# First chunk transposed as fp32 and split into halves on the way out of PSUM, weight slabs in one piece each in DRAM, opening reordered

## The chip, the cores and the metric

The kernel runs on one core of a Trainium2 chip. A core has five engines with instruction queues of their own: TensorE (PE) for matmuls, VectorE (DVE), ScalarE (ACT), GpSimd (POOL) and SyncE (SP), which here issues nearly all DMA transfers. [...] SBUF is the on-chip memory; PSUM holds what TensorE writes, in banks of 128 x 512 fp32.

The metric is the time of one execution in microseconds. Before the change three runs gave 449.02, 449.00 and 449.44 us, median 449.02.

## The reference

Two branches work on the same layer-normalised input and their results are added to it.

```python
xn = (x - mean(x)) / sqrt(var(x) + 1e-5)          # x: 2048 x 448, over the last axis
a  = irfft2(rfft2(xn) * (w_r + 1j * w_i))         # a filter in the frequency domain
b  = (relu(xn @ W_gate) * (xn @ W_up)) @ W_down   # 448 -> 1792 -> 448
out = x + a + b
```

All of it is fp32. The kernel keeps that accuracy with fp16 matmuls: every operand is split into a high half `hi` and a low half `lo`, and a product is hi·hi + lo·hi + hi·lo.

## The kernel before

**Tiling.** The 2048 rows are 16 tiles of 128; tile `n2 = q + 4j` belongs to chunk `q`, so a chunk is four tiles, 512 rows. The chunks are worked on in the order `CHUNKS = [0, 2, 1, 3]`. For each chunk there is a transposed operand `T[q]` (in the records `T_62` for chunk 0) with eight contraction tiles of 128: 0 to 2 hold the high half of the first 384 features, 4 to 6 the low half, and 3 and 7 share the last 64 features, high and low. A ninth tile `Tl` is gathered by small SBUF-to-SBUF transfers (`t_ninth`); the forward transform needs it.

**The gated part.** The 1792 hidden features are 14 slabs `f` of 128, in three groups of 5, 5 and 4. A unit (f, q) of `gu` is two banks, gate (g = 0) and up (g = 1), with ten 128x512 matmuls each (L731), and a pair of units shares four matmuls on half the array (L738, the "halves"). When it is done, ScalarE takes the relu of the gate (L768), VectorE multiplies it by the up bank (L772), ScalarE makes the high half (L776), VectorE the low half (L780). The weights of a slab come as two transfers `wst` (L226) of 256 KB; ScalarE sums their squares (L186), GpSimd reduces over partitions (L189), VectorE makes a scale from it in two steps (L192, L196), ScalarE writes the high half (L681), VectorE the low half (L685). The down projection (`dn`, L799) follows per group and row tile, and VectorE adds its PSUM to the output (L805), which frees the bank. There are two banks each for `gu`, `dn` and `fx` (transforms and transposes).

**The first chunk.** Its rows are loaded (`lx`, L220), VectorE takes the statistics (`st`), ScalarE a square root (`sq`), VectorE makes the reciprocal in five small steps (`rs`), and normalises (`xn`, L293). ScalarE writes the f16 high half from the raw rows (`hi`, L300), GpSimd copies the last 64 columns about (`cp`, L306 and L307), VectorE makes the f16 low half (`lo`, L317 and L318). TensorE transposes eight f16 tiles per row tile against an f16 identity `id_t` (`tpA`, `tpB`, L332), and VectorE or ScalarE copies them out of PSUM into `T` (`vev`, `aev`, L340 and L338). Meanwhile TensorE runs matmuls on a cleared tile (`warm`, 19 of them, and `kw` 1, 6, 3; L1049), whose result is not used. Unit 0 is done in parts of 256 columns (`hh`, `lh`, `hl`, then the gate's or up's number and the half of the chunk), so that it can begin when half of the chunk is there. Chunk 2 goes the old way in both kernels: f16 halves and a transposing DMA (`dm`).

**What sets the order.** The first part is written out by hand: the string `OPENING` names pieces, and each engine's queue gets its share of them in that order (`wsq`, `par`, `wsc`, `whi`, `wlo` for a slab's weight steps, `wdq` for the square sums of the down projection's weights, `re`, `tm`, `gh`, `gl` for the four steps after a unit, `hp` for the halves). Everything behind it is issued unit by unit. A list `bg` holds the transforms, each item with a cost in us on VectorE, and between units as many items are issued as a credit worked out from these costs allows; a scheduler then orders each engine's queue by priorities. Its order also follows what stands in the opening. In the inverse transform a butterfly (L404, L405, L427, L428) feeds a `swap`, two transfers that reverse partitions (L529, L530), and a `pair` (L535, L536) takes the swapped data; in between, rows that need no swap come by small transfers (`y<-row`, L592).

Of the kernel before, what the change touches and what calls it, by code (L numbers as in the profile page):

```python
# [9 lines left out]
F16 = mybir.dt.float16  # L10
F32 = mybir.dt.float32
# [19 lines left out]
lx0 lx4 lw lid lw lx8 lx12 lw lw lw lw lx2 lx10 lx6 lx14 lwd0 lwd1 lwd2 lwd3 lwd4 warm st0 st4 sqA rsA hi4  # L31
xn4 xn0 wsqW0g0 cp4 st8 hi0 parW0g0 st12 wsqW0g1 cp0 tpA0 lo0 tpA4 kw1 wscW0g0 sqB tpB0 kw6 parW0g1 wsqW1g0
rsB whiW0g0 vevB0 lo4 wsqW1g1 xn12 tpB4 kw3 hi8 parW1 wscW0g1 xn8 whiW0g1 cp8 vevA0 vevA4 hi12 tpA8 vevB4
hh10 hh00 lo8 wsqW2g1 cp12 tpA12 hl00 lo12 aevA12 tpB8 aevA8 hl10 wloW0g0 lw aevB8 tpB12 wscW1 lh00 aevB12
wloW0g1 lw lfd hh01 hh11 whiW1g0 st2 lh01 lh10 whiW1g1 hl01 wloW1g0 lw hl11 wsqW2g0 wloW1g1 lw ly0 ly4 ly8
ly12 lh11 wsqW3g0 st10 parW2 hp0 st14 wsqW3g1 gu1g0 st6 wdq0 parW3 wscW2 sqC wscW3 whiW2g0 rsC gu1g1 re0
wloW2g0 whiW3g1 tm0 whiW2g1 xn6 wsqW4g0 xn2 gu2g0 wloW2g1 hi2 re1 xn10 gh0 wloW3g1 whiW3g0 tm1 gu2g1 wdq1
wloW3g0 hi10 xn14 lo2 hi14 hi6 cp14 hp2 wsqW4g1 cp2 lo6 gu3g0 cp10 dm2 lo14 re2 parW4 wdq2 cp6 wscW4 tm2
whiW4g0 dm14 lo10 wdq4 gu3g1 wloW4g0 gh1 dm10 gl0 whiW4g1 gl1 dm6 gu4g0 re3 wloW4g1 wdq3 tm3 wdp gh3
wdsc gh2 gu4g1 gl2 wdh1 wdh2 wdl1 wdh0 wdl2 hp4 gl3 re4 wdh3 tm4 wdl0 gh4 wdh4 gl4 wdl3 wdl4  # L40
# [42 lines left out]
def _constants():  # L83
# [55 lines left out]
    ident = np.eye(128, dtype=np.float16)  # L139
# [5 lines left out]
def tile_gfnet_reglu(ctx: ExitStack, tc: tile.TileContext, x, xr, wgu, wd, wf, ident, c_fd, c_fm, c_im, c_row, c_id,  # L145
# [59 lines left out]
    id_t = ft([128, 128], F16, "id_t")  # L205
# [10 lines left out]
    def load_xr(n2):  # L216

        xr_b[n2] = free.pop(0)
        xr_t[n2] = xr_b[n2].rearrange("p g c k -> p (g c k)")[:, 0:D]
        nc.sync.dma_start(xr_t[n2], xrv[:, n2, :])  # L220
# [34 lines left out]
    rst = {}  # L255
# [21 lines left out]
    for t in tts:  # L277
        G.memset(t[:, 7, 48:64], 0.0)
    for q in CHUNKS:
        G.memset(Tl[q][32:64], 0.0)  # L280

# [4 lines left out]
    def ln_xn(n2, act=False):  # L286
        xn_b[n2] = free.pop(0)
        xn[n2] = xn_b[n2].rearrange("p g c k -> p (g c k)")[:, 0:D]
        r, nm, mean = rst[n2 % 4, n2 // 4]
        if act:  # L290
            A.activation(xn[n2], xr_t[n2], AF.Identity, scale=r, bias=nm)
        else:
            V.tensor_scalar(xn[n2], xr_t[n2], mean, r, op0=OP.subtract, op1=OP.mult)  # L293

    def ln_hi(n2, fused=False):
        new_tt(n2)
        o = tt[n2].rearrange("p a b -> p (a b)")[:, 0:D]
        r, nm, _ = rst[n2 % 4, n2 // 4]
# [29 lines left out]
    def ln_tp(n2, tiles):  # L328
        if n2 not in tp:
            tp[n2] = fx().bitcast(F16).rearrange("p (a b) -> p a b", b=128)  # L330
        for a in tiles:
            P.transpose(tp[n2][:, a, :], tt[n2][:, a, :], id_t)  # L332

    def ln_ev(n2, a0, a1, act):
        q, j = n2 % 4, n2 // 4
        o = Tq[q][:, a0:a1, 128 * j:128 * (j + 1)]
        if act:
            last["A"] = A.activation(o, tp[n2][:, a0:a1], AF.Copy).ins  # L338
        else:
            last["V"] = V.tensor_copy(o, tp[n2][:, a0:a1]).ins  # L340


    def t_ninth(q):

        T = Tq[q]
        with tc.issue_after(last.get("R", last["S"])):
            for r in range(3):
                nc.sync.dma_start(Tl[q][16 * r:16 * (r + 1)], T[112:128, 4 + r])
            nc.sync.dma_start(Tl[q][64:128], T[64:128, 3])
# [701 lines left out]
    pieces = {"lid": lambda: nc.sync.dma_start(id_t, ident), "lfd": lambda: nc.sync.dma_start(fd_t, c_fd),  # L1051
# [8 lines left out]
    for c, q in enumerate(CHUNKS[:2]):  # L1060
        for js, tag in (((0, 1), "A"), ((2, 3), "B")) if c == 0 else (((0, 1, 2, 3), "C"),):
            piece("sq" + tag, ln_sd, q, js)
            piece("rs" + tag, ln_rstd, q, js, c == 0)
        for j in range(4):
            n2 = q + 4 * j
            for tag, fn, *a in (("lx", load_xr), ("ly", load_x), ("st", ln_stats, j), ("xn", ln_xn),
                                ("hi", ln_hi, c == 0), ("cp", ln_copy), ("lo", ln_lo), ("dm", ln_dma),
                                ("tpA", ln_tp, (0, 1, 2)), ("tpB", ln_tp, (4, 5, 6, 3, 7))):
                piece(f"{tag}{n2}", fn, *((q,) if tag == "st" else (n2,)), *a)
            for act in range(2):  # L1070
                piece(f"{'va'[act]}evA{n2}", ln_ev, n2, 0, 3, bool(act))
                piece(f"{'va'[act]}evB{n2}", ln_ev, n2, 3, 8, bool(act))
# [7 lines left out]
    for f in groups[0]:  # L1080
# [5 lines left out]
        piece(f"wscW{f}", w_scale, f)  # L1086
# [4 lines left out]
        for g in range(2):  # L1091
# [4 lines left out]
            if f == 0:  # L1096
                piece(f"parW{f}g{g}", w_sum, f, (g,))
                piece(f"wscW{f}g{g}", w_scale, f, (g,))
# [77 lines left out]
def _arrays(A_x, A_w_r, A_w_i, B_W_gate, B_W_up, B_W_down):  # L1176
# [9 lines left out]
    wgu = np.ascontiguousarray(np.stack([wtiles(B_W_gate), wtiles(B_W_up)], axis=2))  # L1186
# [30 lines left out]
```

## Time and profile before

| | |
|---|---|
| runs | 449.02, 449.00, 449.44 us (median 449.02) |
| profiled execution | 449.44 us, its span 447.6 us |
| TensorE busy | 437.9 us (98%), granted clock 0.998 |
| VectorE busy | 387.2 us (87%) |
| ScalarE busy | 186.7 us (42%) |
| GpSimd busy | 28.8 us (6%) |
| DMA | 39.54 MB, mean 88 GB/s |

The span is the time from the first to the last instruction in the trace; the execution has 1.84 us around it. A row of a timeline has the start in us, the duration, the engine, the line, the operation with its tiles, and in brackets how long the engine had been idle and what released it; `x6` is a run of six such instructions with their common duration. Busy shares are averages over stages with different limits, so the rows of a stage count, not the page's total.

### The profile page before, as it was taken

How to read it: one execution, taken by the hardware profiler on the slowest of the kernel's cores; microseconds unless marked ns; L12 is line 12 of the kernel's file. 1: busy time of each engine (PE TensorE's matmuls, PEld its weight loads, DVE VectorE, ACT ScalarE, POOL GpSimd, SP SyncE). 2: the span in 40 equal slices, each digit the busy share in tenths (PEclk: the TensorE clock that was granted, in tenths of full speed). 3: DMA queues.
4: the chain of work that ended last, by engine and by line, in shares of the span. 5: the costliest groups of instructions: out<-in, count | busy, mean ns of one | idle time of the engine just before them, and what ended most of it. 6: DMA issues, size and time to landing. Idle time of an engine off the chain costs nothing.

```text
span 447.6 us, 7353 instructions
## 1 busy us (share of the span) xinstructions
PE 437.9 (98%) x2616; PEld 218.8 (49%) x2616; DVE 387.2 (87%) x958; ACT 186.7 (42%) x398; POOL 28.8 (6%) x77
## 2 busy tenths in 40 slices
PE   6999999999999999999999999999999999999996
PEld 2644645545445444444444444444445555555653
DVE  5999779777969998999999999999789799699753
ACT  5896263742553955133124255344214134134230
POOL 4220020200100140000000000000000000000000
PEclk9999999999999999999999999999999999999999
DMA  7828985400001272412220210001011211211212
GB/s 259 313 68 246 320 334 105 96 0 22 2 1 48 95 243 74 132 54 72 84 84 2 83 41 1 1 1 61 23 41 55 68 34 56 89 34 48 94 63 82
DMA packets 37756, 39.54 MB, mean 88 GB/s; under 512 B 16550, under 2 KB 33624, under 8 KB 37720
## 3 DMA queue, kind: packets, MB, share of 16 engines
q1 hardware_dynamic: 37720, 39.09, 28.0%
q8 instruction: 20, 0.33, 0.3%
q14 instruction: 16, 0.13, 0.1%
HBM read 24.38 MB, written 3.67 MB: 63 GB/s over the span
## 4 chain that ended last, share of the span: by engine, by line
PE 52%; DVE 38%; DMA 3%; issue 3%; ACT 2%; POOL 1%; SPq 1%; DVEq 0%; ACTq 0%; POOLq 0%
PE gu L731 26%; PE dn L799 12%; DVE g L772 3%; DVE h L780 3%; DVE wt L685 3%; DVE xy L805 2%; PE fx L630 2%; PE fx L649 2%; DVE y L502 2%; DVE y L503 2%; DVE y L405 2%; DVE y L404 2%; DMA sw<-y 2%; DVE y L427 2%; PE gu L738 2%
## 5 line engine op out<-in xcount | busy, mean ns | idle before, releaser
L731 PE MATMUL gu<-T,wt 128*128 128x512 f16 (+1 forms) x1140 | 255.0, 375 | 0.0
L731 PEld LDWEIGHTS <-wt 128*128 128x128 f16 x1140 | 108.8, 98 | 128.3 <-issue 8.5
L799 PE MATMUL dn<-wdt,h 128*128 128x448 f16 x624 | 127.1, 352 | 0.3 <-DVE xy L805 0.3
L799 PEld LDWEIGHTS <-h 128*128 128x128 f16 x624 | 60.3, 98 | 57.7 <-issue 1.1
L776 ACT ACTIVATE h<-g 128x512 f16<-128x512 f32 x56 | 35.0, 627 | 78.8 <-DVE g L772 78.6
L768 ACT ACTIVATE g<-gu 128x512 f32<-128x512 f32 x56 | 33.0, 589 | 73.7 <-PE gu L738 52.1
L772 DVE SCALAR_TENSOR_TENSOR g<-gu,g 128x512 f32<-128x512 f32 x56 | 38.2, 682 | 4.2 <-ACT g L768 4.2
L780 DVE TENSOR_TENSOR h<-g,h 128x512 f16<-128x512 f32 x56 | 38.2, 683 | 3.1 <-ACT h L776 2.6
L805 DVE SCALAR_TENSOR_TENSOR xy<-dn,dsc,xy 128x448 f32<-128x448 f32 x44 | 29.8, 678 | 6.2 <-PE dn L799 6.2
L614 ACT ACTIVATE vt<-y,fsc 128x456 f16<-128x456 f32 x16 | 10.8, 672 | 29.9 <-PE fx L630 17.4
L681 ACT ACTIVATE wt<-wst,wsc 128x512 f16<-128x512 f32 x28 | 19.0, 714 | 6.2 <-DVE wsc L196 6.2
L189 POOL PARTITION_ALL_REDUCE wm<-wm x15 | 9.3, 617 | 181.9 <-ACT junk L186 161.8
L654 DVE SCALAR_TENSOR_TENSOR xy<-fx,fsc,xy 128x448 f32<-128x448 f32 x16 | 10.9, 679 | 11.0 <-PE fx L649 10.9
L685 DVE SCALAR_TENSOR_TENSOR wt<-wst,wsc,wt 128x512 f16<-128x512 f32 x28 | 20.2, 744 | 0.1
L738 PE MATMUL gu<-T,wt 64*128 64x512 f16 x112 | 17.0, 381 | 1.6 <-DVE g L772 1.4
L535 DVE TENSOR_TENSOR y<-y,sw 128x228 f32<-128x228 f32 x32 | 12.4, 388 | 6.8 <-DMA sw<-y 4.1
L186 ACT ACTIVATE junk<-wst 128x512 bf16<-128x512 f32 x28 | 17.4, 622 | 1.3 <-DMA wst<-in_wgu 1.0
L405 DVE TENSOR_TENSOR y<-y,y 128x456 f32<-128x456 f32 x22 | 13.8, 628 | 1.7 <-DMA row<-y 1.4
L392 DVE TENSOR_TENSOR Xh<-X,Xh 128x456 f16<-128x456 f32 x16 | 9.9, 626 | 5.8 <-ACT Xh L389 5.7
L404 DVE TENSOR_TENSOR y<-y,y 128x456 f32<-128x456 f32 x22 | 13.8, 628 | 0.4
L630 PE MATMUL fx<-im,vt 128*128 128x128 f16 x192 | 13.5, 219 | 0.0
L389 ACT ACTIVATE Xh<-X 128x456 f16<-128x456 f32 x16 | 9.2, 577 | 10.1 <-DVE X L387 8.9
(128 smaller groups left out, 476.2 us busy)
## 6 DMA issues: line engine op xcount, KB each, us to landing
sw<-y SPq DMA_DIRECT2D x64, 112.2 KB
wst<-in_wgu SPq DMA_DIRECT2D x28, 256.0 KB
wf<-in_wf SPq DMA_DIRECT2D x16, 228.0 KB
y<-in_xr SPq DMA_DIRECT2D x16, 224.0 KB
xy<-in_x SPq DMA_DIRECT2D x16, 224.0 KB
out<-xy SPq DMA_DIRECT2D x15, 224.0 KB
wdst<-in_wd SPq DMA_DIRECT2D x14, 224.0 KB
fm<-in_c_fm SPq DMA_DIRECT2D x4, 256.0 KB
```

The lines of the kernel that those rows point to most:

```text
L404: V.tensor_tensor(t, a, b, op=OP.add)
L405: V.tensor_tensor(b, a, b, op=OP.subtract)
L630: P.matmul(o, v[:, h, w], m[:, c, :], start=(i == 0), stop=(i == 2), skip_group_check=True)
L685: V.scalar_tensor_tensor(w[:, 4:8, :], st, sc, w[:, 0:4, :], op0=OP.mult, op1=OP.subtract)
L731: last["P"] = P.matmul(hps[f, q][:, g, cs], wt[f, g][:, a, :], Tq[q][:, b, cs], start=(start and i == 0), stop=(stop and i == len(seq) - 1 ...
L738: m = P.matmul(hps[f, q][:, g, 0:512], wt[f, g][rows, 7, :], Tq[q][rows, b, :], start=start, stop=not start).ins
L768: last["A"] = A.activation(g1s[f, q], hps[f, q][:, 0, :], AF.Relu, scale=2.0 ** -22).ins
L772: last["V"] = V.scalar_tensor_tensor(g1, hps[f, q][:, 1, :], 2.0 ** -22, g1, op0=OP.mult, op1=OP.mult).ins
L776: A.activation(ht[f, q][:, 0, :], g1s[f, q], AF.Copy)
L780: V.tensor_tensor(h[:, 1, :], g1s.pop((f, q)), h[:, 0, :], op=OP.subtract)
L799: last["P"] = P.matmul(ps[:, 0:D], ht[f, q][:, a, js], wdt[f][:, b, :], start=(i == 0), stop=(i == n - 1)).ins
L805: last["V"] = V.scalar_tensor_tensor(xy[:, n2, :], dps[n2][:, 0:D], dsc[:, g:g + 1], xy[:, n2, :], op0=OP.mult, op1=OP.add).ins
```

## The change

**First chunk.** The normalised rows are written as fp32 into the memory of the f16 tiles (`xw`), VectorE as before; ScalarE copies the last 64 columns a second time behind them (`xd`). TensorE transposes four fp32 tiles per row tile (16 instead of 32 in all) against an fp32 identity (64 KB instead of 32). ScalarE writes the high half out of PSUM (`th`, 128x4x128, and `tu`, 64x128), and VectorE the low half as PSUM minus high half (`tl`, 128x3x128, and `tv`, 64x128). The f16 halves, the GpSimd copies and the f16 evacuations of this chunk are gone. Tile 7 of `T` now gets its missing rows by three more small transfers in `t_ninth`, and is cleared ahead by one more memset of 32x512; the four memsets of the f16 tiles move behind the transposes.

**Weights.** `wgu` is laid out slab by slab and half by half, so that a transfer of 256 KB reads one piece of DRAM.

**Order.** The identity is loaded from ScalarE's queue. The five steps of the reciprocal and the two of the scale are pieces of their own, and `OPENING` is another string. On TensorE it gives: 20 warm-ups, 8 transposes, 9 warm-ups, 3 matmuls of 128x256, 8 transposes, 37 matmuls of 128x256, where it was 19 warm-ups, then transposes in groups of 3 to 6 with warm-ups or matmuls of 128x256 between them.

Three places, in each engine's queue. First ScalarE in the opening, from unit 0's first high half on; `wt` is a weight's high half, `junk,wm` a square sum, `T_62` the transposed chunk. Before:

```order
L681 ACTIVATE wt<-wst,wsc 128x512
L186 ACTIVATE junk,wm<-wst 128x512
L300 ACTIVATE tt_105<-y_72,rs 128x448
L681 ACTIVATE wt<-wst,wsc 128x512
L300 ACTIVATE tt_106<-y_73,rs 128x448
L186 ACTIVATE junk,wm<-wst 128x512
L338 ACTIVATE T_62<-fx 128x3x128 x2
L338 ACTIVATE T_62<-fx 128x5x128 x2
L681 ACTIVATE wt<-wst,wsc 128x512 x2
```

After, same place:

```order
L356 ACTIVATE T_62<-fx 64x128
L354 ACTIVATE T_62<-fx 128x4x128
L342 ACTIVATE tt_106<-tt_106 128x64
L342 ACTIVATE tt_105<-tt_105 128x64
L190 ACTIVATE junk,wm<-wst 128x512
L708 ACTIVATE wt<-wst,wsc 128x512
L190 ACTIVATE junk,wm<-wst 128x512
L356 ACTIVATE T_62<-fx 64x128
L354 ACTIVATE T_62<-fx 128x4x128
```

All four tiles now leave PSUM through ScalarE, in pairs of a small and a large piece, where it took two of the four before.

Second, ScalarE around 30 us, ahead of slab 4's high half, the last `wt` in each list (`wdm` is a square sum of the down projection's weights, `g` the relu of a unit). Before:

```order
L681 ACTIVATE wt<-wst,wsc 128x512
L186 ACTIVATE junk,wdm<-wdst 128x448
L302 ACTIVATE tt_104<-y_84 128x448
L302 ACTIVATE tt_105<-y_85 128x448
L302 ACTIVATE tt_106<-y_82 128x448
L186 ACTIVATE junk,wm<-wst 128x512
L768 ACTIVATE g_513<-gu 128x512
L186 ACTIVATE junk,wdm<-wdst 128x448
L681 ACTIVATE wt<-wst,wsc 128x512
```

After:

```order
L190 ACTIVATE junk,wdm<-wdst 128x448
L708 ACTIVATE wt<-wst,wsc 128x512
L306 ACTIVATE tt_104<-y_79 128x448
L803 ACTIVATE h<-g_394 128x512
L306 ACTIVATE tt_105<-y_81 128x448
L190 ACTIVATE junk,wm<-wst 128x512
L190 ACTIVATE junk,wdm<-wdst 128x448
L306 ACTIVATE tt_106<-y_80 128x448
L190 ACTIVATE junk,wdm<-wdst 128x448
L795 ACTIVATE g_489<-gu 128x512
L708 ACTIVATE wt<-wst,wsc 128x512 x2
```

The high half now stands behind three square sums of the down projection in this stretch, where it stood behind two, and directly behind the relu.

Third, VectorE where the inverse transform first needs swapped data, near 316 us (`y<-y,sw` are the pairs, `g` a gate product, `xy<-dn` the evacuation of the down projection). Before:

```order
L588 TENSOR_SCALAR row<-fx,small 16x4x57 x2
L780 TENSOR_TENSOR h<-g_3465,h 128x512
L535 TENSOR_TENSOR y_77<-y_77,sw_1904 128x4x57
L536 TENSOR_TENSOR y_77<-y_77,sw_1904 128x4x57
L602 TENSOR_TENSOR y_70<-y_77 128x228
L603 TENSOR_TENSOR y_77<-y_77 128x228
L604 TENSOR_TENSOR y_77<-y_77 128x114
L772 SCALAR_TENSOR_TENSOR g_3506<-gu,g_3506 128x512
L605 TENSOR_TENSOR y_77<-y_77 128x114
L535 TENSOR_TENSOR y_79<-y_79,sw_1905 128x4x57
L536 TENSOR_TENSOR y_79<-y_79,sw_1905 128x4x57
L805 SCALAR_TENSOR_TENSOR xy<-dn,dsc,xy 128x448
```

After:

```order
L613 TENSOR_SCALAR row<-fx,small 16x4x57 x2
L453 SCALAR_TENSOR_TENSOR y_81<-y_70,y_81 128x456
L807 TENSOR_TENSOR h<-g_3446,h 128x512
L560 TENSOR_TENSOR y_77<-y_77,sw_1885 128x4x57
L561 TENSOR_TENSOR y_77<-y_77,sw_1885 128x4x57
L832 SCALAR_TENSOR_TENSOR xy<-dn,dsc,xy 128x448
L799 SCALAR_TENSOR_TENSOR g_3487<-gu,g_3487 128x512
L560 TENSOR_TENSOR y_83<-y_83,sw_1886 128x4x57
L561 TENSOR_TENSOR y_83<-y_83,sw_1886 128x4x57
```

The evacuation moved up, to directly behind the first pair. Some 30 instructions later in the same queue the gate product of the next unit stood like this before, the pair with `sw_1904` being the one that waited 18 instructions ahead of it:

```order
L535 TENSOR_TENSOR y_74<-y_74,sw_1904 128x4x57
L536 TENSOR_TENSOR y_74<-y_74,sw_1904 128x4x57
L780 TENSOR_TENSOR h<-g_3649,h 128x512
L602 TENSOR_TENSOR y_77<-y_75 128x228
L805 SCALAR_TENSOR_TENSOR xy<-dn,dsc,xy 128x448
```

and stands like this after, one row ahead of the pair with the same swap (`sw_1885`):

```order
L645 SCALAR_TENSOR_TENSOR vt_1882<-y_83,fsc,vt_1882 128x456
L628 TENSOR_TENSOR y_75<-y_75 128x228
L560 TENSOR_TENSOR y_81<-y_81,sw_1888 128x4x57
L561 TENSOR_TENSOR y_81<-y_81,sw_1888 128x4x57
L799 SCALAR_TENSOR_TENSOR g_3630<-gu,g_3630 128x512
L560 TENSOR_TENSOR y_74<-y_74,sw_1885 128x4x57
```

The product moved from behind that pair to ahead of it.

The diff, cut to its core (of `OPENING` the first line of each):

```diff
 OPENING = """
-lx0 lx4 lw lid lw lx8 lx12 lw lw lw lw lx2 lx10 lx6 lx14 lwd0 lwd1 lwd2 lwd3 lwd4 warm st0 st4 sqA rsA hi4
...
+lx0 lx4 lw st0 lx8 lx12 lw lw lw lwd2 lid lw lw lwd0 st4 lwd1
...
-    ident = np.eye(128, dtype=np.float16)
+    ident = np.eye(128, dtype=np.float32)
...
-    id_t = ft([128, 128], F16, "id_t")
+    id_t = ft([128, 128], F32, "id_t")
...
-        eng.dma_start(wst[f, g], wgu[f, :, g])
+        eng.dma_start(wst[f, g], wgu[f, g])
...
-    for t in tts:
-        G.memset(t[:, 7, 48:64], 0.0)
     for q in CHUNKS:
         G.memset(Tl[q][32:64], 0.0)
+    G.memset(Tq[CHUNKS[0]][32:64, 7], 0.0)
...
-    def ln_tp(n2, tiles):
-        if n2 not in tp:
-            tp[n2] = fx().bitcast(F16).rearrange("p (a b) -> p a b", b=128)
-        for a in tiles:
-            P.transpose(tp[n2][:, a, :], tt[n2][:, a, :], id_t)
-
-    def ln_ev(n2, a0, a1, act):
+    xw = {CHUNKS[0] + 4 * j: t.rearrange("p a b -> p (a b)").bitcast(F32) for j, t in enumerate(tts)}
+
+    def ln_xw(n2, act=False):
+        r, nm, mean = rn[n2 % 4, n2 // 4]
+        if act:
+            A.activation(xw[n2][:, 0:D], xr_t[n2], AF.Identity, scale=r, bias=nm)
+        else:
+            V.tensor_scalar(xw[n2][:, 0:D], xr_t[n2], mean, r, op0=OP.subtract, op1=OP.mult)
+
+    def ln_xd(n2):
+        A.activation(xw[n2][:, 448:512], xw[n2][:, 384:448], AF.Copy)
+
+    def ln_tp(n2):
+        tp[n2] = fx().rearrange("p (a b) -> p a b", b=128)
+        for a in range(4):
+            P.transpose(tp[n2][:, a, :], xw[n2][:, 128 * a:128 * (a + 1)], id_t)
+        G.memset(tts[n2 // 4][:, 7, 48:64], 0.0)
+
+    def ln_thi(n2, part):
         q, j = n2 % 4, n2 // 4
-        o = Tq[q][:, a0:a1, 128 * j:128 * (j + 1)]
-        if act:
-            last["A"] = A.activation(o, tp[n2][:, a0:a1], AF.Copy).ins
+        T, js = Tq[q], slice(128 * j, 128 * (j + 1))
+        if part == 0:
+            A.activation(T[:, 0:4, js], tp[n2], AF.Copy)
         else:
-            last["V"] = V.tensor_copy(o, tp[n2][:, a0:a1]).ins
-
+            last["A"] = A.activation(T[64:128, 7, js], tp[n2][64:128, 3], AF.Copy).ins
+
+    def ln_tlo(n2, part):
+        q, j = n2 % 4, n2 // 4
+        T, js = Tq[q], slice(128 * j, 128 * (j + 1))
+        if part == 0:
+            V.tensor_tensor(T[:, 4:7, js], tp[n2][:, 0:3], T[:, 0:3, js], op=OP.subtract)
+        else:
+            last["V"] = V.tensor_tensor(T[64:128, 3, js], tp[n2][64:128, 3], T[64:128, 7, js], op=OP.subtract).ins
...
                 nc.sync.dma_start(Tl[q][16 * r:16 * (r + 1)], T[112:128, 4 + r])
+                if q == CHUNKS[0]:
+                    nc.sync.dma_start(T[16 * r:16 * (r + 1), 7], T[112:128, r])
...
-    pieces = {"lid": lambda: nc.sync.dma_start(id_t, ident), "lfd": lambda: nc.sync.dma_start(fd_t, c_fd),
+    pieces = {"root": lambda: A.activation(mt([128, 1], F32, "root"), eps, AF.Sqrt),
+              "lid": lambda: nc.scalar.dma_start(id_t, ident), "lfd": lambda: nc.sync.dma_start(fd_t, c_fd),
...
-    wgu = np.ascontiguousarray(np.stack([wtiles(B_W_gate), wtiles(B_W_up)], axis=2))
+    wgu = np.ascontiguousarray(np.stack([wtiles(B_W_gate), wtiles(B_W_up)], axis=1))
```

More of the change, by code (lines that the diff above doesn't have):

```diff
@@ L253, in ln_stats @@
         V.bn_aggr(mv[q][:, j, :], st)
-    rst = {}
+    rst, rn = {}, {}
     def ln_sd(q, js=(0, 1, 2, 3)):
@@ L297, in ln_hi @@
         o = tt[n2].rearrange("p a b -> p (a b)")[:, 0:D]
[L298 removed]
+        r, nm, _ = rn[n2 % 4, n2 // 4]
         if fused:
@@ L1085, in tile_gfnet_reglu @@
         piece(f"parW{f}", w_sum, f)
-        piece(f"wscW{f}", w_scale, f)
+        for k in range(2):
+            piece(f"wscW{f}.{k}", w_scale, f, (0, 1), k)
         for tag, fn in (("re", gu_relu), ("tm", gu_times), ("gh", gu_hi), ("gl", gu_lo)):
@@ L1097, in tile_gfnet_reglu @@
                 piece(f"parW{f}g{g}", w_sum, f, (g,))
-                piece(f"wscW{f}g{g}", w_scale, f, (g,))
+                for k in range(2):
+                    piece(f"wscW{f}g{g}.{k}", w_scale, f, (g,), k)
                 for h in range(2):
```

75 lines of the change are left out of this document (40 added, 35 removed).

## Prediction

> **What bounds the kernel now.** I read the page first: the busy line, the granted clock, the shares of the chain that ended last, and the two matmul groups that show any idle time.
>
> ```profile
> span 447.6 us, 7353 instructions
> ...
> PE 437.9 (98%) x2616; PEld 218.8 (49%) x2616; DVE 387.2 (87%) x958; ACT 186.7 (42%) x398; POOL 28.8 (6%) x77
> ...
> PEclk9999999999999999999999999999999999999999
> ...
> PE 52%; DVE 38%; DMA 3%; issue 3%; ACT 2%; POOL 1%; SPq 1%; DVEq 0%; ACTq 0%; POOLq 0%
> ...
> L799 PE MATMUL dn<-wdt,h 128*128 128x448 f16 x624 | 127.1, 352 | 0.3 <-DVE xy L805 0.3
> ...
> L738 PE MATMUL gu<-T,wt 64*128 64x512 f16 x112 | 17.0, 381 | 1.6 <-DVE g L772 1.4
> ```
>
> TensorE is busy for 98% of the span at a full granted clock, so the time is TensorE's work plus the few places where TensorE has nothing to do. Idle time in the middle is 0.3 and 1.6 us. Then I cut the span into stretches, with each engine's busy time in each.
>
> ```profile
> 0.00:20.00 20.00, 15.80 (x105) 9.14 (x105) 14.63 (x48) 13.73 (x29) 6.86 (x25) 1.00 0.86 293
> ...
> 40.00:160.00 120.00, 120.00 (x740) 60.67 (x739) 99.37 (x276) 60.21 (x130) 12.70 (x29) 1.00 0.38 113
> 160.00:310.00 150.00, 150.00 (x742) 68.21 (x740) 145.66 (x326) 57.48 (x136) 5.95 (x12) 1.00 0.20 61
> 310.00:340.00 30.00, 28.32 (x148) 13.36 (x147) 25.52 (x65) 8.31 (x14) 0.00 (x0) 1.00 0.12 39
> ```
>
> The columns after the length are busy time on TensorE, its weight loads, VectorE, ScalarE and GpSimd. From 40 to 310 us TensorE never stops; from 160 to 310 VectorE is full too (145.66 of 150). So the change can act in two places: in the first 20 us, where TensorE still runs warm-up matmuls and waits for the first chunk, and around 310 to 340 us, where 30 − 28.32 = 1.7 us are lost. The matmuls of the two projections and the transforms stay as they are in number and shape.
>
> **The opening, term by term.** The rows are the timeline's: start, busy time, engine, line.
>
> ```profile
> 0.74 0.24 POOL L278 MEMSET tt<- 128x16 f16 x4 [0.29 <-POOLq L1205]
> ...
> 1.03 1.90 POOL L280 MEMSET Tl<- 32x512 f16 x4
> ...
> 3.58 6.97 PE L1049 MATMUL dn<-warm 128*128 128x512 f16 x19 [3.58 <-POOL warm L1106]
> ...
> 10.93 0.44 PE L332 MATMUL fx<-id_t,tt 128*128 128x128 f16 x5
> ...
> 11.21 1.46 PE L1049 MATMUL dn<-warm 128*128 128x512 f16 x6
> ...
> 14.21 0.81 PE L731 MATMUL gu<-T,wt 128*128 128x256 f16 x6
> ...
> 16.54 3.01 PE L731 MATMUL gu<-T,wt 128*128 128x256 f16 x26
> ...
> 19.73 0.61 PE L738 MATMUL gu<-T,wt 64*128 64x512 f16 x4 [0.18 <-DVE wt L685]
> ...
> 29.55 6.65 PE L731 MATMUL gu<-T,wt 128*128 128x512 f16 x30
> ```
>
> *Start.* GpSimd no longer clears four strips ahead (1.03 − 0.74 = 0.29 us less) and clears one more 32x512 strip (1.90/4 = 0.48 more). The warm-up matmuls wait for the memset behind it, so TensorE starts 0.19 later, at 3.77. Twenty warm-ups instead of 19 end at 3.77 + 6.97 + 0.22 = 10.96 (a warm 128x512 is 6.65/30 = 0.22).
>
> *The transposes.* No row shows an fp32 one. From below: an f16 one takes (11.21 − 10.93)/5 = 0.056. From above: the warm 128x512 matmul, which streams four times the columns, 0.22. I take 0.12: the tile to be transposed is the stationary operand and used once, it has twice the bytes of an f16 tile, and twice 0.056 is 0.112. Each engine's program has 16 of them where it had 32, so at 0.12 they cost 1.92 in place of 1.79. [...]
>
> *To the first projection matmul.* Eight transposes (0.96) and nine warm-ups (1.98) follow: 10.96 + 0.96 + 1.98 = 13.90, against 14.21.
>
> *To the end of unit 0,* the row at 19.73. Forty 128x256 matmuls at 3.01/26 = 0.116 (4.63) and the other eight transposes (0.96) give 19.49 if nothing waits. ScalarE decides whether something does: the later half-chunk needs its four evacuations. Rows for its prices, the first three with mean nanoseconds behind the busy time:
>
> ```profile
> L681 ACT ACTIVATE wt<-wst,wsc 128x512 f16<-128x512 f32 x28 | 19.0, 714 | 6.2 <-DVE wsc L196 6.2
> ...
> L768 ACT ACTIVATE g<-gu 128x512 f32<-128x512 f32 x56 | 33.0, 589 | 73.7 <-PE gu L738 52.1
> ...
> L186 ACT ACTIVATE junk<-wst 128x512 bf16<-128x512 f32 x28 | 17.4, 622 | 1.3 <-DMA wst<-in_wgu 1.0
> ...
> 15.04 0.19 ACT L186 ACTIVATION_READ_ACCUMULATOR junk<-wst 128x1 f32 x1
> ```
>
> From the first finished transposes (10.96 + 4 × 0.12 = 11.44) it runs four 128x512 evacuations out of PSUM (0.589 each by the gate's row, 2.36), four small 64x128 ones and two 128x64 copies (six at about 0.2, the small row, 1.2), two square sums (2 × 0.75 after the overlap of the two rows, 1.5) and one weight half (0.71): 5.77 us, to 17.2. TensorE gets to the later half-chunk after 17 matmuls and the eight transposes, at 13.90 + 1.97 + 0.96 = 16.83. That is a wait of up to 0.4; since ScalarE's operations overlap at their ends, I take 0.2. Unit 0 then ends at 19.7, where it ended before: **0.0**. With the transposes at 0.056 ScalarE's end would move by 0.26 only, so the gain stops at 0.3. At 0.22, TensorE is 16 × 0.10 = 1.6 later and the wait of 0.2 is gone: +1.4.
>
> What goes with it is off the path: four ScalarE and eight GpSimd operations and eight f16 evacuations leave, and VectorE's low halves come straight out of PSUM; VectorE has 14.63 of 20 us there. The identity's transfer goes from SyncE's queue to ScalarE's, twice as large, ahead of the table load; the row tiles behind it land earlier by one transfer. Neither is waited for at 10.96.
>
> **Slab 4's weights.** ScalarE is ordered anew around 30 us.
>
> ```profile
> 29.75 0.61 ACT L186 ACTIVATE junk<-wst 128x512 bf16<-128x512 f32 x1
> ...
> 30.83 0.56 ACT L186 ACTIVATE junk<-wdst 128x448 bf16<-128x448 f32 x1
> ...
> 32.01 0.72 ACT L681 ACTIVATE wt<-wst,wsc 128x512 f16<-128x512 f32 x1 [0.52 <-DVE wsc L196]
> ...
> 33.09 0.75 DVE L685 SCALAR_TENSOR_TENSOR wt<-wst,wsc,wt 128x512 f16<-128x512 f32 x1
> ```
>
> Slab 4's first matmul comes 20 matmuls after 29.55, at 33.99; its low half was done at 33.84, so the cover is 0.15. In the new order one more square sum of the down projection (0.56 + 0.19 = 0.75) stands ahead of slab 4's high half. Of that the 0.52 in which ScalarE waited for the scale can absorb all or nothing: the low half comes 0.23 to 0.75 later, and TensorE waits 0.1 to 0.6. I take **+0.4**, as the re-ordered VectorE queue gives no reason for the kind end.
>
> **310 to 340 us.** The rest of the kernel is ordered by the scheduler, and its order changes though the work does not.
>
> ```profile
> 305.63 0.67 DVE L772 SCALAR_TENSOR_TENSOR g<-gu,g 128x512 f32<-128x512 f32 x1
> ...
> 306.87 0.71 SPq L529 DMA_DIRECT2D sw<-y  x1
> ...
> 313.61 12.22 SPq L592 DMA_DIRECT2D y<-row  x5
> ...
> 315.92 0.40 DVE L535 TENSOR_TENSOR y<-y,sw 128x228 f32<-128x228 f32 x1 [2.65 <-DMA y<-row]
> ...
> 319.23 0.68 DVE L805 SCALAR_TENSOR_TENSOR xy<-dn,dsc,xy 128x448 f32<-128x448 f32 x1
> ...
> 319.96 5.83 PE L799 MATMUL dn<-wdt,h 128*128 128x448 f16 x30 [0.29 <-DVE xy L805]
> ...
> 329.45 0.40 DVE L535 TENSOR_TENSOR y<-y,sw 128x228 f32<-128x228 f32 x1 [1.42 <-DMA sw<-y]
> ...
> 336.16 0.61 PE L738 MATMUL gu<-T,wt 64*128 64x512 f16 x4 [1.40 <-DVE g L772]
> ```
>
> SyncE issues eight swap transfers in (313.61 − 306.87) = 6.74 us, 0.84 each, and a row behind them; VectorE stands 2.65 us at the first pair that needs the row, and the evacuation that frees the down projection's PSUM (L805) stands behind it. TensorE lost 0.29 there. In the new order that evacuation comes directly behind the first pair, the butterfly that feeds the first swap comes eight VectorE instructions later behind the same gate product (145.66/326 = 0.45 each, 3.6 us), and six swaps instead of eight stand ahead of the row (−1.7). The first pair is then ready 315.92 + 3.6 − 1.7 = 317.8 and the evacuation done 1.3 later, at 319.1, just in time for TensorE at 319.7, if the gate product itself comes when it did. VectorE is full up to there, and each microsecond by which it is further behind goes into TensorE's wait beyond the first 0.6. Bounds: nothing, and VectorE's whole 2.65. I take 1.6, nearer to the 2.65, because nothing stands between pair and evacuation any more that would soften a delay.
>
> The second stall goes the other way. Before, the gate product of the next unit stood 18 instructions behind the pair that waited 1.42 us; in the new order it stands one row ahead of such a pair. The 1.40 can go wholly; I leave 0.3 of it. So 1.6 + 0.3 = 1.9 in place of 0.29 + 1.40 = 1.69: **+0.2**, between −1.7 and +2.4.
>
> **Parts at nothing.** Weight slabs in one piece: only 1.0 us in the whole run waits for such a transfer (the square sum's row above, of 28), and from 40 us on the transfer engines are busy 0.38 or less. The three added 16-row moves into the first chunk's ninth tile:
>
> ```profile
> 39.49 1.87 SPq L348 DMA_DIRECT2D Tl<-T  x3
> ...
> 48.34 0.72 PE L361 MATMUL fx<-fd_t,T 128*128 128x114 f16 x11
> ```
>
> Three cost SyncE 1.87 us; three more shift the queue by as much, and the tail they feed is used seven microseconds later.
>
> **Sum.** 0.0 + 0.4 + 0.2 = +0.6 on the profiled execution's 449.44 (span 447.6 and 1.84 around it). That was the highest of the three runs, 0.42 over their median of 449.02; as a median I forecast 449.6. A measurement of this kernel can tell about 0.2%, 0.9 us, from no change, so this is within it, on the slow side.
>
> **Rivals.** *Faster, the stalls close:* slab 4's weights come in time (the kind end, 0.1), the evacuation is early enough at 319.7, and the gate product no longer stands behind the pair. Its place is VectorE at 305 us; it decides once the product there comes no more than 0.6 later than before. For it: the worked-out 319.1 above. Against: VectorE's 97% up to that point. 449.02 − 1.7 and 0 to 0.3 for the opening: 447.2. Chance 0.26.
>
> *The transposes at their upper end:* its place is TensorE between 10.96 and 19.5, and it decides from about 0.17 each, where 16 × 0.05 = 0.8 is added. For it: no row shows TensorE reading fp32 at all, so the f16 spacing may not carry over. Against: the array's busy rows follow columns, and these are 128 wide as before. 449.6 + 1.4 = 451.0. Chance 0.16. [...]
>
> *The row's wait reaches TensorE whole:* 2.65 instead of 1.6, and the gate stall stays: 449.02 + 0.4 + 2.4 = 451.8. For it, the queue of swaps is issued one by one; against, two fewer are ahead. Chance 0.12.
>
> *Likeliest, near 449.6,* own range 448.4 to 450.8: 0.46. Of it 0.30 lies within 0.2% (448.1 to 449.9), 0.11 above, 0.05 below. Together: faster 0.05 + 0.24 of the first rival = 0.29; same 0.30 + 0.02 = 0.32; slower 0.11 + 0.16 + 0.12 = 0.39. The range reaches from the first rival's 447.2 nearly to the last one's, 451.5.
>
> **What would show it.** The fp32 transposes' spacing in the timeline between the 20 and the 9 warm-ups (0.12, 1 us for eight); the first 128x256 matmul at about 13.9 and the unit's half-array matmuls at about 19.7; a wait for the weight's low half at about 34; one wait of 1 to 2 us on the evacuation at about 320 and a small one on the gate product behind it. The forecast is wrong if the eight transposes take nearly 2 us, if TensorE waits for ScalarE by far more than 0.4 in the opening, or if a stall shows in 40 to 310 us, where there was none.

## The result, and the profile after

The changed kernel takes 452.13 us (median of 4 runs, 451.39 to 453.06), the kernel before 449.15 in the same comparison: ratio 1.0065, 95% interval 1.0053 to 1.0078, **slower** by 3.0 us, 0.65%. The profiled execution took 451.81 us, its span is 450.0. The forecast was 449.6.

The page of the changed kernel, the lines that answer to those of before (lines of code from 360 on stand 25 to 28 further down: L731 is L758 now, L738 is L765, L772 is L799, L799 is L826, L805 is L832):

```profile
span 450.0 us, 7307 instructions
...
PE 438.5 (97%) x2600; PEld 218.6 (49%) x2600; DVE 386.3 (86%) x955; ACT 184.7 (41%) x402; POOL 28.5 (6%) x70
...
L758 PE MATMUL gu<-T,wt 128*128 128x512 f16 (+1 forms) x1140 | 255.0, 375 | 1.5 <-DVE g L799 1.0
...
L826 PE MATMUL dn<-wdt,h 128*128 128x448 f16 x624 | 127.0, 352 | 2.4 <-DVE xy L832 2.0
...
L765 PE MATMUL gu<-T,wt 64*128 64x512 f16 x112 | 17.0, 381 | 0.2 <-DVE g L799 0.2
```

The work is the same. The stall in front of the halves (1.6 us before) is almost gone, and in its place `gu` waits 1.5 and `dn` 2.4 us. The stretches, with the columns as before the change, say where:

```profile
0.00:20.00 20.00, 15.86 (x90) 9.14 (x91) 13.87 (x44) 13.74 (x36) 5.35 (x18) 1.00 0.92 321
...
40.00:160.00 120.00, 120.00 (x741) 60.74 (x740) 98.62 (x274) 59.85 (x131) 9.97 (x22) 1.00 0.37 110
160.00:310.00 150.00, 148.54 (x730) 67.43 (x730) 141.88 (x319) 56.79 (x135) 9.21 (x19) 1.00 0.21 62
310.00:340.00 30.00, 27.92 (x139) 12.79 (x138) 26.43 (x64) 7.07 (x14) 0.00 (x0) 1.00 0.15 47
```

From 160 to 310 us, where TensorE had been busy without a break, 1.46 us are lost, and between 310 and 340 it loses 2.08 where it lost 1.68. VectorE did 145.66 us of work in 160 to 310 before and does 141.88 now: it idles 3.8 us more, and what it did not do there it does later. The timeline of the changed kernel, from the opening to the last stall:

```profile
3.75 6.79 PE L1076 MATMUL dn<-warm 128*128 128x512 f16 x20 [3.75 <-POOL warm L1134]
...
10.37 1.04 PE L347 MATMUL fx<-id_t,tt 128*128 128x128 f32 x8
...
11.24 2.11 PE L1076 MATMUL dn<-warm 128*128 128x512 f16 x9
...
13.19 0.49 PE L758 MATMUL gu<-T,wt 128*128 128x256 f16 x3
...
16.78 2.67 PE L758 MATMUL gu<-T,wt 128*128 128x256 f16 x23 [0.30 <-ACT T L354]
...
19.38 0.60 PE L765 MATMUL gu<-T,wt 64*128 64x512 f16 x4
...
24.60 4.48 PE L758 MATMUL gu<-T,wt 128*128 128x512 f16 x20 [0.19 <-DVE g L799]
29.01 0.61 PE L765 MATMUL gu<-T,wt 64*128 64x512 f16 x4
...
194.18 3.18 PE L758 MATMUL gu<-T,wt 128*128 128x512 f16 x14 [0.77 <-DVE g L799]
...
275.90 1.12 PE L826 MATMUL dn<-wdt,h 128*128 128x448 f16 x5 [0.42 <-ACT h L803]
...
322.71 1.48 PE L826 MATMUL dn<-wdt,h 128*128 128x448 f16 x7 [1.98 <-DVE xy L832]
```

The opening is 0.35 us shorter (unit 0's halves at 19.38, before at 19.73). The wait at 24.60 takes that back, and the next halves stand at 29.01 in both executions; before:

```profile
29.01 0.61 PE L738 MATMUL gu<-T,wt 64*128 64x512 f16 x4
```

All by which the changed kernel is behind at its end is lost from 194 us on, 170 us behind the code that was changed. What VectorE waited for between 160 and 325 us (us in total, times, longest), before:

```profile
DVE y L535 <- DMA y<-row: 2.6, 1, 2.6
DVE y L535 <- DMA sw<-y: 1.7, 2, 1.1
```

and in the changed kernel:

```profile
DVE y L560 <- DMA sw<-y: 2.7, 3, 1.3
DVE y L560 <- DMA y<-row: 2.7, 1, 2.7
DVE y L430 <- DMA row<-y: 1.5, 1, 1.5
DVE h L807 <- ACT h L803: 1.1, 2, 0.9
DVE y L465 <- PE fx L423: 0.2, 1, 0.2
```

4.3 us before, 8.2 after, of which 6.9 for transfers. The row's wait (2.6 and 2.7 us) is in both; from 160 to 310 us alone it is 1.7 before and 5.5 after. Three of the waits, 3.7 us in all, come ahead of the first stall of TensorE, where the kernel before has its two of 1.09 and 0.65 us (at 178.93 and 184.30):

```profile
167.40 0.63 DVE L430 TENSOR_TENSOR y<-y,y 128x456 f32<-128x456 f32 x1 [1.47 <-DMA row<-y]
...
184.47 0.40 DVE L560 TENSOR_TENSOR y<-y,sw 128x228 f32<-128x228 f32 x1 [1.26 <-DMA sw<-y]
...
189.63 0.40 DVE L560 TENSOR_TENSOR y<-y,sw 128x228 f32<-128x228 f32 x1 [0.95 <-DMA sw<-y]
```

### The profile page after: what moved, and what is told of

Its sections match the earlier page's. It is cut to its first block, busy times and chain, and to the rows that moved or that the text cites. A ratio compares the mean times of both kernels' runs of the same rounds, so it can differ in the third digit from the quotient of the medians.

```text
span 450.0 us, 7307 instructions
## 1 busy us (share of the span) xinstructions
PE 438.5 (97%) x2600; PEld 218.6 (49%) x2600; DVE 386.3 (86%) x955; ACT 184.7 (41%) x402; POOL 28.5 (6%) x70
## 4 chain that ended last, share of the span: by engine, by line
PE 57%; DVE 25%; issue 7%; DMA 4%; ACT 3%; POOL 2%; SPq 1%; POOLq 0%; DVEq 0%; ACTq 0%
PE gu L758 29%; PE dn L826 14%; PE fx L655 2%; DVE g L799 2%; PE fx L386 2%; PE fx L674 2%; DVE xy L832 2%; PE fx L423 2%; DMA sw<-y 2%; DVE h L807 2%; PE gu L765 2%; DVE y L430 2%; PE dn L1076 2%; DVE y L452 1%; DVE y L527 1%
## 5 line engine op out<-in xcount | busy, mean ns | idle before, releaser
L758 PE MATMUL gu<-T,wt 128*128 128x512 f16 (+1 forms) x1140 | 255.0, 375 | 1.5 <-DVE g L799 1.0
L758 PEld LDWEIGHTS <-wt 128*128 128x128 f16 x1140 | 108.9, 98 | 131.4 <-issue 12.0
L826 PE MATMUL dn<-wdt,h 128*128 128x448 f16 x624 | 127.0, 352 | 2.4 <-DVE xy L832 2.0
L826 PEld LDWEIGHTS <-h 128*128 128x128 f16 x624 | 60.4, 98 | 60.0 <-issue 2.7
L799 DVE SCALAR_TENSOR_TENSOR g<-gu,g 128x512 f32<-128x512 f32 x56 | 38.2, 682 | 7.0 <-ACT g L795 6.9
L832 DVE SCALAR_TENSOR_TENSOR xy<-dn,dsc,xy 128x448 f32<-128x448 f32 x44 | 29.8, 677 | 6.6 <-PE dn L826 6.5
L765 PE MATMUL gu<-T,wt 64*128 64x512 f16 x112 | 17.0, 381 | 0.2 <-DVE g L799 0.2
L674 PEld LDWEIGHTS <-pgh 114*128 114x128 f16 x192 | 11.0, 98 | 3.9 <-issue 0.8
L453 DVE SCALAR_TENSOR_TENSOR y<-y,y 128x456 f32<-128x456 f32 x20 | 12.5, 626 | 0.3
```

The lines of the kernel that those rows point to most:

```text
L674: P.matmul(ps[:, o], h[:, a, i, :], idc_t[:, b, o], start=(j == 0), stop=(j == 2), skip_group_check=True)
L758: last["P"] = P.matmul(hps[f, q][:, g, cs], wt[f, g][:, a, :], Tq[q][:, b, cs], start=(start and i == 0), stop=(stop and i == len(seq) - 1 ...
L765: m = P.matmul(hps[f, q][:, g, 0:512], wt[f, g][rows, 7, :], Tq[q][rows, b, :], start=start, stop=not start).ins
L799: last["V"] = V.scalar_tensor_tensor(g1, hps[f, q][:, 1, :], 2.0 ** -22, g1, op0=OP.mult, op1=OP.mult).ins
L826: last["P"] = P.matmul(ps[:, 0:D], ht[f, q][:, a, js], wdt[f][:, b, :], start=(i == 0), stop=(i == n - 1)).ins
L832: last["V"] = V.scalar_tensor_tensor(xy[:, n2, :], dps[n2][:, 0:D], dsc[:, g:g + 1], xy[:, n2, :], op0=OP.mult, op1=OP.add).ins
```

## The experiments

Two theories at first. **Order:** the loss is what the scheduler made of the queues behind the opening; their instructions are the same. **Parts:** the loss comes from a part of the change itself, the fp32 transposes, the added transfers, ScalarE's evacuations or the slabs. The kernel before reads 449.15, 449.08, 448.80 and 449.18 us in the four comparisons, so times from different comparisons are set side by side by their ratios to it.

### Opening and order apart

The traced instructions behind the opening are the same in both kernels, apart from the three added transfers, so each can be held to the order of the other by tying every instruction to the one ahead of it on its engine. First the changed kernel with the old order behind its opening.

```diff
+QUEUES = {"PE": ..., "DVE": ..., "Activation": ..., "Pool": ..., "SP": ...}
...
+            for a, b in zip(row, row[1:]):
+                tc.add_manual_dep(b, a.name, mybir.DependencyInfo(mybir.DependencyClass.NoSync, mybir.DependencyReason.DATA),
+                                  reason="imposed order")
```

> The changed kernel with its whole opening, its slab layout and its three added transfers, but with every engine's queue behind the opening held to the order of the kernel before. Theory 'order' (the loss is what the scheduler did to the queues behind the opening): stalls of about 1.7 us at 320 and 336 us as before, none at 194 and 276, unit 0's halves at 19.4, and a time 0.2 to 0.5 us under the kernel before, near 448.8. Rival 'parts' (the loss comes from the change's own parts: fp32 transposes, added transfers, ScalarE's new load): it stays slower, near 452.

Measured: 448.65 (11 runs) against 449.08 for the kernel before (27 runs), ratio 0.9988, interval 0.9979 to 0.9997. Then the reverse, the old kernel with the changed kernel's order:

> The kernel before with its own opening and layout, but with every engine's queue behind the opening held to the order of the changed kernel. Theory 'order': slower by about what the changed kernel is, plus the 0.35 us that its opening does not gain: 452.0 to 452.8, with the stalls at about 194, 276 and 322 us. Rival 'parts': as the kernel before, 449.2, within 0.5.

Measured: 452.04 (5 runs, 451.14 to 453.09), ratio 1.0068, interval 1.0054 to 1.0082. TensorE's waits in that kernel:

```profile
...
PE dn L886 <- DVE xy L892: 1.6, 1, 1.6
PE dn L886 <- ACT h L863: 0.5, 1, 0.5
...
PE gu L818 <- DVE g L859: 0.4, 1, 0.4
...
```

So the old opening with the new order is as slow as the changed kernel, and the changed opening with the old order is a little faster than the kernel before. All the loss is the order. In the old order the change's own parts gain about 0.5 us by the ratio (0.1 to 0.9 by its interval); in the new order the two openings can't be told apart (1.0068 and 1.0065). Which of the five queues' orders makes the loss is not separated by these two kernels. The wait at 336 us is still there with the old order, at 1.3 us.

```profile
...
PE gu L850 <- DVE g L884: 1.3, 1, 1.3
...
```

The slabs alone, with every queue in its old order:

```diff
-        eng.dma_start(wst[f, g], wgu[f, :, g])
+        eng.dma_start(wst[f, g], wgu[f, g])
...
-    wgu = np.ascontiguousarray(np.stack([wtiles(B_W_gate), wtiles(B_W_up)], axis=2))
+    wgu = np.ascontiguousarray(np.stack([wtiles(B_W_gate), wtiles(B_W_up)], axis=1))
```

> The kernel before with the weight slabs in one piece each and nothing else; every queue's order is as before. Both theories: within 0.2% of the kernel before (449.2, at most 0.3 off), since 1 us in all waited for such a transfer. A rival 'layout' (contiguous slabs land at another time and collide with the row transfers) would show 1 us or more.

Measured: 448.93 against 449.08, ratio 0.9996, interval 0.9988 to 1.0005. Nothing that can be told from none.

### What in the opening turns the order

The orders of rebuilt kernels, without any run, narrow it down: with another number of warm-ups in the kernel before, with the changed kernel's order of free row buffers, without the three added transfers or with the old slabs in the changed kernel, the queues behind the opening come out as they were. With the last pieces of the opening in another order they don't.

```diff
-cp6 tm2 gl0 whiW4g1 gu3g0 dm14 wloW4g0 dm6 gh1 wdq3 lo10 wdp dm10 gl1 gu3g1 gu4g0
-re3 wloW4g1 tm3 wdsc wdh3 wdl3 wdh2 gu4g1 wdh4 wdh1 hp4 re4 wdl1 tm4 gh3 wdl2
-wdh0 gh2 gl3 gh4 wdl4 wdl0 gl2 gl4
+cp6 tm2 gl0 whiW4g1 gu3g0 dm14 wloW4g0 dm6 gh1 wdq3 lo10 dm10 gl1 gu3g1 gu4g0
+re3 wloW4g1 tm3 wdp gh3
+wdsc gh2 gu4g1 gl2 wdh1 wdh2 wdl1 wdh0 wdl2 hp4 gl3 re4 wdh3 tm4 wdl0 gh4 wdh4 gl4 wdl3 wdl4
```

> The changed kernel with the last pieces of its opening (the third-last line from one piece on, and the last two) in the order that the kernel before had them; the pieces are the same. The scheduler then gives a third order: on VectorE 324 lines differ from the changed kernel's and 263 from that of the kernel before. Theory 'order': the time is another draw, anywhere from 447.5 to 452.5, with its own stalls behind 160 us and the opening as in the changed kernel (unit 0's halves at 19.4). Rival 'parts': 452, as the changed kernel, within 0.5.

Measured: 448.12 (11 runs) against 448.80 (23 runs), ratio 0.9992, interval 0.9983 to 1.0002: by the ratios 3.3 us under the changed kernel, and not to be told from the kernel before, by moving pieces at 35 to 45 us, where TensorE has no stall with either order. It is a third order and not the old one, so these pieces turn the order but are not all that sets it. In 160 to 310 us VectorE works 145.30 us there and TensorE 149.86:

```profile
160.00:310.00 150.00, 149.86 (x739) 68.25 (x738) 145.30 (x324) 58.09 (x136) 6.16 (x13) 1.00 0.19 59
```

### Why TensorE waits: the place in the queue, or a VectorE without slack

At 321 us VectorE stands 2.69 us before the first pair while the evacuation and the gate product that TensorE needs are ready behind it. Three instructions are moved ahead of that pair, in the order of the changed kernel:

```diff
 TENSOR_TENSOR h<-g_3446,h
+SCALAR_TENSOR_TENSOR xy<-dn,dsc,xy x2
+SCALAR_TENSOR_TENSOR g_3487<-gu,g_3487
 TENSOR_TENSOR y_77<-y_77,sw_1885
 TENSOR_TENSOR y_77<-y_77,sw_1885
-SCALAR_TENSOR_TENSOR xy<-dn,dsc,xy
-SCALAR_TENSOR_TENSOR g_3487<-gu,g_3487
 TENSOR_TENSOR y_83<-y_83,sw_1886
 TENSOR_TENSOR y_83<-y_83,sw_1886
 TENSOR_TENSOR y_70<-y_77
-SCALAR_TENSOR_TENSOR xy<-dn,dsc,xy
```

> The changed kernel with three VectorE instructions moved: the two evacuations of the down projection and the gate product that stood behind the first pair at 321 us stand ahead of it, in the 2.7 us in which VectorE waits for the row transfer; all else as in the changed kernel. Theory 'place in the queue' (TensorE's 1.98 us there is the evacuation standing behind a waiting pair, nothing more): the stall at 322 goes and the time falls by 1.5 to 2.0, to about 450.3. Rival 'VectorE is the bound' (it is behind anyway, and what is gained at 322 is lost again at the next gate product, 336): the time falls by less than 0.7.

Measured: 450.19 (11 runs), ratio 1.0025, interval 1.0015 to 1.0036, where the changed kernel had 1.0065, so 1.8 us less. The stall at 322 is gone, and of 30 us TensorE is busy for 29.77:

```profile
310.00:340.00 30.00, 29.77 (x158) 13.81 (x157) 28.34 (x71) 8.23 (x15) 0.00 (x0) 1.00 0.15 47
```

Then the same at 194 and 275 us, where a gate product is moved ahead as well:

> The changed kernel with five VectorE instructions moved: the three at 321 us as in the run before, and two gate products that TensorE waited for, at 194 us (moved ahead of the pair that waits 0.95 us for its swap) and at 275 us (moved ahead of six butterfly and filter steps). Theory 'place in the queue': the 0.8 to 1.0 us at 194 and the 0.45 at 276 go too, and the time falls from 450.2 to about 449.0, the time of the kernel before. Rival 'VectorE is the bound': what is moved ahead pushes the butterflies back, the stalls come again a few us later and the time stays within 0.5 of 450.2.

Measured: 449.93 (11 runs), ratio 1.0024, interval 1.0015 to 1.0033: no gain over the run above. The waits for gate products shrink (the one at 194, 1.04 us in the run above, is gone), and others come a few us later, such as 0.92 us at 206:

```profile
...
PE dn L913 <- ACT h L890: 0.9, 1, 0.9
PE gu L852 <- DVE g L886: 0.5, 2, 0.2
...
PE dn L913 <- DVE h L894: 0.5, 1, 0.5
...
```

Here the rival held: in that stretch VectorE itself is late, and moving one instruction ahead makes another late. To see it from the other side, VectorE is given slack in the changed kernel's order:

```diff
-        V.tensor_tensor(t, xt, bc[0], op=OP.mult)
-        V.tensor_tensor(xt, xt, bc[1], op=OP.mult)
+        V.tensor_tensor(t[:, 0:1], xt[:, 0:1], bc[0][:, 0:1], op=OP.mult)
+        V.tensor_tensor(xt[:, 0:1], xt[:, 0:1], bc[1][:, 0:1], op=OP.mult)
```

> The changed kernel, every queue in its own order, but with the 32 multiplications by the frequency filter on VectorE (L527, L528) done on a quarter of their columns; the rest of the filter's product is left out. That takes about 32 x 0.36 = 11 us off VectorE between 180 and 310 us and nothing off TensorE. Theory 'VectorE full' (the new stalls at 194, 228, 234 and 276 us come from a VectorE without slack, which any reordering tips over): they vanish, the one at 322 shrinks since the swaps are issued earlier, and the time is 449.0 to 450.2. Rival 'order alone' (TensorE waits because an instruction stands behind another's wait for a transfer, however much slack VectorE has): the stalls stay, 451.5 to 452.5.

Measured: 448.37 (12 runs) against 449.18 (23 runs), ratio 0.9982, interval 0.9972 to 0.9992, lower than expected. The stalls at 228, 234, 276 and 322 us are gone. The one at 194 is not; it is even longer, 1.2 us:

```profile
...
PE gu L845 <- DVE g L886: 1.4, 2, 1.2
...
```

The first of the shortened multiplications stands at 190.59, so there was hardly any slack yet and this run can't say what slack would do at 194. The pairs' waits (1.26 and 0.95 us above) and the place of the product behind them are its likely cause, since the stall was gone with the product moved ahead. Both theories have their stretch: 'place in the queue' at 322, where VectorE stands waiting, and 'VectorE full' from 228 to 276.

### A version that beats both, and what the opening is worth

The same moves in the old order: the two evacuations and the product ahead of the first pair at 316 us, and the gate product of 336 us moved up to three instructions behind the pair it waited for.

> The kernel before with the same four VectorE instructions moved and its own opening. Theory 'place in the queue': 449.08 less 1.4 to 1.7, near 447.6; what it lies above the same order with the changed opening is what that opening is worth, 0.2 to 0.4 us. If the changed opening is worth nothing the two are equal within 0.1.

> The changed kernel's opening, the queues behind it in the order of the kernel before, and four VectorE instructions moved: the two evacuations and the product behind the first pair at 316 us stand ahead of it, and the gate product that TensorE waits 1.3 us for at 336 us stands three instructions behind the pair it waited for instead of 18. Theory 'place in the queue': 448.65 less 1.3 is 447.3, under both kernels. Rival 'VectorE is the bound': 448.3 to 448.7, the stall moved on.

Measured in one comparison against 448.80 (23 runs): with the old opening 447.56 (7 runs), ratio 0.9973, interval 0.9962 to 0.9983; with the changed opening **447.26** (5 runs, 446.86 to 447.54), ratio 0.9966, interval 0.9954 to 0.9979, the fastest of all. By the ratios the moves gain 1.2 us in the kernel before, where 1.4 to 1.7 was expected, and 1.0 us on top of the changed opening, where 1.3 was. That both medians still meet the times forecast is luck: the kernel before was 0.3 us faster in this comparison. Behind the opening TensorE does not wait any more for anything but 0.2 us at 24. The changed opening is worth 0.3 here and 0.5 above; the intervals of the two kernels overlap, so its size is no better known than that.

Is the opening one chain, so that TensorE's time in it counts? In the fastest kernel each fp32 transpose is issued twice:

```diff
             P.transpose(tp[n2][:, a, :], xw[n2][:, 128 * a:128 * (a + 1)], id_t)
+            P.transpose(tp[n2][:, a, :], xw[n2][:, 128 * a:128 * (a + 1)], id_t)
```

> The fastest kernel so far (changed opening, queues behind it as before, four VectorE instructions moved; 447.3) with each of the 16 fp32 transposes issued twice. Theory 'the opening is one chain' (TensorE and ScalarE have no slack up to unit 0's end): 16 x 0.11 = 1.8 us slower at most, less up to 0.7 where TensorE waits for VectorE or ScalarE anyway: 448.3 to 449.0. Rival 'covered' (the first chunk waits for loads and statistics, not for TensorE): within 0.4 of 447.3.

Measured: 448.70 (12 runs) against 449.18, ratio 0.9989, interval 0.9979 to 0.9999. By the ratios that is 0.0023, 1.0 us, more than without; by the medians, each set against the kernel before in its comparison, 1.1. It counts, less what TensorE waits for there anyway: in the fastest kernel that is 0.43 us for VectorE between the later eight transposes, a wait that is gone here. The added transposes stand 0.11 us apart, as the first ones do.

## Why the prediction was wrong

**The start and the transposes** held. TensorE starts at 3.75 (3.77 said), and eight transposes take from 10.37 to 11.24, 0.109 each (0.12 said, from twice the f16 spacing). By these traces an fp32 transpose takes 0.109 us where the f16 one took 0.056, twice as long. Whether that is the bytes of the stationary tile, as I argued, or the fp32 identity that streams, no run here separates.

**Unit 0's end** at 19.7 came at 19.38, and that it came so near is in part luck, as two errors go against each other. The twenty warm-ups ended at 10.4, not at 10.96, as their weight loads stood 0.22 us apart from 8.41 on, and in the execution of before only from 9.09 on, 0.7 us later, which is chance (below). From the first projection matmul to unit 0's end it then took 6.19 us where the sum had 5.8. The wait for ScalarE's half was 0.30 (0.2 said), and the second eight transposes took 1.27 (13.51 to 14.78) and not 0.96; the sum had no wait for VectorE there. Over many runs the opening gains 0.3 to 0.5, where the sum had 0.0.

**Slab 4's weights, +0.4,** fell. There is no wait at 34 us. The sum counted one more square sum ahead of the high half but not that the square sum which the scale waits for had also moved: it runs at 28.83 where it ran at 29.75, so ScalarE no longer stood still for the scale, and the low half was there at 33.73.

```profile
28.83 0.62 ACT L190 ACTIVATE junk<-wst 128x512 bf16<-128x512 f32 x1
...
31.65 1.32 ACT L708 ACTIVATE wt<-wst,wsc 128x512 f16<-128x512 f32 x2
...
32.99 0.74 DVE L712 SCALAR_TENSOR_TENSOR wt<-wst,wsc,wt 128x512 f16<-128x512 f32 x1
```

In its place came 0.19 us at 24.60, which the sum had not. It stands in all eight traces with the changed opening and in none of the four with the old one, and took back what the profiled opening had gained.

**310 to 340 us** was right in its mechanism and a little small in size: 1.98 at the evacuation where I took 1.6, and the gate product's stall gone where I left 0.3. The product came later than I let it:

```profile
308.90 0.68 DVE L799 SCALAR_TENSOR_TENSOR g<-gu,g 128x512 f32<-128x512 f32 x1
...
313.95 0.71 SPq L554 DMA_DIRECT2D sw<-y  x1
...
321.24 0.40 DVE L560 TENSOR_TENSOR y<-y,sw 128x228 f32<-128x228 f32 x1 [2.69 <-DMA y<-row]
...
321.98 0.68 DVE L832 SCALAR_TENSOR_TENSOR xy<-dn,dsc,xy 128x448 f32<-128x448 f32 x1
```

308.90, that is 3.3 us behind the 305.63 of before; it was named as the condition ("if the gate product itself comes when it did") and not worked out. With these 3.3 us the first pair, worked out for 317.8, comes at 321.1; it came at 321.24.

**The step that failed** is the sentence that the change can act in two places, the first 20 us and 310 to 340. The sum has no term for 160 to 310 us, although the prediction itself read there that VectorE was full. I took a stretch without stalls for one that a new order could not hurt; it was the stretch with the least slack. The new order puts pairs and joins on VectorE before their transfers have landed (5.5 us of waits in that stretch, 4.2 of them for transfers, where there were 1.7), the lateness is not made up because 145 of 150 us are work, and TensorE pays 0.77, 0.16, 0.10 and 0.42 us on the way and 1.98 at the end. The runs bear the parts of that out: order alone makes the loss (452.04 with the old opening), and slack on VectorE takes all of it away but the first stall. The prediction did name a stall in 40 to 310 us as a sign that it is wrong, but gave it neither a term nor a chance. The rival that came nearest in time, the row's wait reaching TensorE whole (451.8), had 1.98 of its 2.65 and did not have its other half, a gate stall that stays; its chance of 0.12 was too low for want of the same term.

The account of the two profiled executions: at 29.01 they are level, so all of the 2.37 between 449.44 and 451.81 lies behind that. The recorded stalls there are 3.43 against 1.69 us, +1.74. They are a little too short, because a row of matmuls in the trace reaches past the start of the next. In the kernel before, for one, the second of these rows begins 0.17 us ahead of the end of the first, without any wait:

```profile
38.83 4.49 PE L731 MATMUL gu<-T,wt 128*128 128x512 f16 x20
43.15 0.54 PE L799 MATMUL dn<-wdt,h 128*128 128x448 f16 x2
```

If each recorded wait lacks as much, the five of the changed kernel and the two of before differ by 0.5 more. By this estimate 2.2 of the 2.37 are placed, and the rest stays open. Nor is it shown why the slow order's runs spread over 2 us (451.1 to 453.1) and those of the fastest kernel over 0.7; that its waits hang on when transfers land would fit, and was not tried.

## What to carry to other kernels

Where a scheduler orders the queues, a change in one stage is a new order for all the stages behind it; compare the orders along the whole kernel, and look first at the stretches where an engine beside the bottleneck is full, since a stall-free row there says nothing about slack. Judge a change with the rest of the order held fixed, as the two crossed kernels do here; otherwise its own gain (0.3 to 0.5 us) drowns in the draw of the scheduler (+3.0 in one order; within 0.2 us of the old order, by the ratios, in another that came of moving a few pieces). Where an engine stands waiting for a transfer, put the instructions that the bottleneck needs ahead of the wait: three or four moved rows were worth 1.0 to 1.8 us. The same kind of move where that engine was late already, at 194 and 275 us, was worth nothing, as the wait came again elsewhere.

## What the runs showed of the hardware that I had not expected

The moment at which TensorE goes from one 128x512 matmul in 0.43 us to one in 0.22 us changes from one execution to the next by up to 3 us. The same 20 warm-up matmuls, started at the same time, in the fastest kernel and in the one with doubled transposes, each with the two rows of its weight loads between which the spacing goes from 0.43 to 0.22 us:

```profile
3.75 5.90 PE L1161 MATMUL dn<-warm 128*128 128x512 f16 x20 [3.75 <-POOL warm L1219]
...
6.28 0.15 PEld L1161 LDWEIGHTS <-warm 128*128 128x128 f16 x1 [0.28 <-issue]
6.68 2.47 PEld L1161 LDWEIGHTS <-warm 128*128 128x128 f16 x12 [0.25 <-issue]
```

```profile
3.75 7.38 PE L1162 MATMUL dn<-warm 128*128 128x512 f16 x20 [3.75 <-POOL warm L1220]
...
9.27 0.15 PEld L1162 LDWEIGHTS <-warm 128*128 128x128 f16 x1 [0.28 <-issue]
9.67 0.96 PEld L1162 LDWEIGHTS <-warm 128*128 128x128 f16 x5 [0.25 <-issue]
```

In the first the weight loads were 0.22 us apart from 6.68 on, in the second from 9.67 on; among the twelve traces of this case the change came 2.9 to 5.9 us after the first matmul, with the granted clock shown as 1.00 over the first 20 us (before, after, after_thin and transp_twice). The end of the warm-ups moves with it, by 1.5 us between these two. Unit 0's halves stand at 18.86 to 19.71 in the seven traces with the changed opening and single transposes, so two single executions cannot be compared in their openings to better than 0.9 us. What sets the moment no run here shows.
